# Layer one's paired blocks: one minimum from VectorE to ScalarE, weight conversion packed into five groups of eight, four subtractions to GpSimd, and 896 instead of 1,280 warming columns

## The chip, the cores and the metric

The kernel runs on one core of a Trainium2 chip, in one launch. Times are device microseconds (us) of that core, first as a median over runs without a profiler; beside them stands one execution that the hardware profiler recorded, which all rows come from. Engines are named as the profile names them: PE is TensorE's matmuls, PEld its weight loads, DVE VectorE, ACT ScalarE, POOL GpSimd, SP the queue that issues most DMAs.

## The reference

What is computed is a long convolution followed by two dense layers, each with a hidden width of 2,048:

```
X = np.fft.rfft(x, axis=1)                    # x: 2 x 3008 x 256
y = np.fft.irfft(X * F, n=3008, axis=1)       # F = filt_r + 1j * filt_i
x1 = y.reshape(6016, 256)
h = x1 @ w_in                                 # layer one, 256 -> 2048
g = np.where(h > 0, h, np.exp(np.minimum(h, 0)) - 1)
x2 = g @ w_out                                # 2048 -> 256
h2 = x2 @ w2_in                               # layer two
out = (h2 * np.clip(h2 + 3, 0, 6) / 6) @ w2_out
```

Inputs are float32, and the weights are handed over as 64-bit floats and converted on the chip.

## The kernel before, in words

**Products in three passes.** A dense product is made with operands split into a high and a low part: `mm3` (L88, L89, L90) issues three matmuls of up to 512 columns into one PSUM bank. ACT rounds the high part (L84, L559, L674), DVE subtracts it from the value for the low part (L85, L564, L679).

**Stages.** The prologue transforms the first half of the input (`s1t` L158, `tr` L171, `s2_mm` L202, `i2_mm` L222, `i1_mm` L245). Ahead of it `WARM` multiplies a tile of zeros (L1022), a list of column counts, one float32 matmul each. Then come 128 *units* (three blocks of layer one together, then five single ones), each with 12 matmuls, and last 64 *groups*. A unit's or group's extra jobs hang in slots: `at(pre, n, ...)` puts a call into slot n, a unit has one slot, a group four, and a slot's calls are issued in program order at that place. All engines run their own list in order.

**Pairs and groups.** Two blocks make a pair and share seven products instead of eight (Strassen). Layer one has two pairs, layer two six; a pair takes eight groups. Each group computes seven products (`prod`) and eight second products (`second`), 15 times three matmuls, for four hidden tiles called (0,0), (1,1), (1,0) and (0,1). Their operands are sums of input halves: `x_sums` (L548) makes four subtractions per pair, t1 to t4, and `x_high` and `x_low` (L559, L564) split them. For layer one's first pair this happens during the last single block, for the others in groups 2 to 8 of the pair before.

**The gate of layer one.** For a hidden tile h the gate is max(h, exp(min(h,0)) - 1). `add` (L634) makes h on DVE out of PSUM. For tiles in `LATE` DVE then takes min(h, 0) (L637) and `relu` issues only an exponential on ACT (L654). For others ACT takes relu(-h) (L650) and then exp of its negative (L658). `gate` (L666) joins both on DVE, `high` and `low` split the result, and `second` multiplies it.

**Conversion.** `w_chain2` is a generator that turns layer two's 64-bit weights into two float32 parts and sums of them, one piece per step: L295 to L306, L326, L373 on ACT and DVE, and L321, L330, L354, L365, L375 on POOL or DVE, as `helper` decides. `helper(1)` is POOL while the unit counter `place[0]` is from 88 to 126, DVE otherwise; the counter stops at 128 (`NU`) when groups begin. Of 101 steps, 76 are placed in units and 25 (`LEFT`) in layer one's pairs.

Of the kernel before, what the change touches and what calls it, by code (L numbers as in the profile page):

```python
# [32 lines left out]
ROUNDS = [(l, p) for l in range(2) for p in range(len(PAIRS[l]))]  # L33
# [14 lines left out]
def fft_conv_moe_moe2(ctx, tc, xp, fq, sg, cs1, cs1t, cs2, ci2, ci1, ident, w1i, w1o, w2i, w2o, out):  # L48
    nc = tc.nc
# [18 lines left out]
    def t2(shape, dt=F32):  # L68
        return p2.tile(shape, dt, tag="t2", name=name("t2"))

    def bank():
        return ps.tile([P, 512], F32, tag="ps", name=name("ps"))
# [31 lines left out]
    def got(acc, n):  # L104
        return acc[:, :n] if n == 512 else sorted_(acc[:, :n])

    def like(t, n):
        return t[:, :n] if n == 512 else halves_of(t[:, :n])
# [177 lines left out]
    def helper(layer):  # L286
        first, last = HELP[layer]
        return nc.gpsimd if first <= place[0] < last else nc.vector
# [130 lines left out]
    def w_chain2(fetch):  # L419
        bits, pending = w_words(1, 0), None  # L420
        next(bits)
        yield
        for f in range(NF + 2):
            if f < NF:
                for _ in range(2):
                    next(bits)
                    yield
                next(bits)
                if f + 1 < NF:
                    following = w_words(1, f + 1)  # L430
                    next(following)
                next(bits)
                fetch(f + 2)
                yield
                w_join(f)
                bits = following
            if 0 < f <= NF:
                w_high(f - 1)
            if pending:
                next(pending)  # L440
            yield
            if 0 < f <= NF:
                w_low(f - 1)
            if pending:
                next(pending)
                pending = None
            yield
            if f and f % 2 == 0:
                pending = w_sums(1, f // 2 - 1)
                for _ in range(2):  # L450
                    next(pending)
                    yield
# [86 lines left out]
    def x_sums(l, p, i):  # L539
        n = WIDTHS[l, p]  # L540
        if i == 0:
            xt[l, p] = [t2([P, 512]) for _ in range(4)]
        b11, b21 = (xb[l, p, 0][:, c, :n] for c in range(2))
        b12, b22 = (xb[l, p, 1][:, c, :n] for c in range(2))
        t1, t2_, t3, t4_ = (t[:, :n] for t in xt[l, p])
        out, a, b = ((t1, b12, b11), (t2_, b22, t1), (t3, b22, b12), (t4_, b21, t2_))[i]
        eng = nc.vector if (l, p) in ROUNDS[:4] else nc.gpsimd
        eng.tensor_tensor(out=out, in0=a, in1=b, op=ALU.subtract)  # L548

    def x_source(l, p, m):  # L550
# [64 lines left out]
                queue = nc.scalar if last and s else nc.sync  # L615
                queue.dma_start(out[d * P : (d + 1) * P, t0 + s : t0 + e], t[:, : e - s])

    LATE = ((0, 1), (1, 1))

    class Group:  # L620
        def __init__(self, l, p, q):
# [9 lines left out]
        def add(self, key, u, bank_):  # L631
            n = self.n
            self.h[key] = t2([P, 512])
            nc.vector.tensor_tensor(out=like(self.h[key], n), in0=got(bank_, n), in1=like(u, n), op=ALU.add)  # L634
            if not self.l and key in LATE:
                self.g[key] = t2([P, 512])
# [5 lines left out]
        def relu(self, key):  # L642
# [4 lines left out]
            if self.l:  # L647
                nc.scalar.activation(like(r, n), h, AF.Relu, bias=three)  # L648
            elif key not in LATE:
                nc.scalar.activation(like(r, n), h, AF.Relu, scale=-1.0)  # L650
# [167 lines left out]
    NU = len(units)  # L818

    NS = NU + 4 * (NF // 2) * len(ROUNDS)  # L820
    pre = [[] for _ in range(NS)]
    post = [[] for _ in range(NU + 8)]

    def at(slots, n, fn, *args):
        slots[n].append(lambda: fn(*args))
# [15 lines left out]

    WLEAD = 1

    WARM = (512, 512, 256)

# [24 lines left out]
    for n in range(NI, span):  # L872
        k = -(-n_steps * (n + 1 - NI) // (span - NI)) - done
# [8 lines left out]
    conv2 = w_chain2(fetch2)  # L882
    GROUPS = NF // 2
# [25 lines left out]
    L2 = NU + 4 * GROUPS * len(PAIRS[0])  # L909
# [5 lines left out]
    for first, last, number in ((50, 58, 10), (62, 88, 4), (88, NU - 1, 62)):  # L915
        k0 = 0
        for n in range(first, last):
            k = number * (n + 1 - first) // (last - first) - k0
# [1 line left out]
            k0 += k  # L920
        DONE += number
    LEFT = 101 - DONE
    LAST = L2 - 4
    done2 = 0
    for n in range(NU, LAST):
        k = -(-LEFT * (n + 1 - NU) // (LAST - NU)) - done2
        at(pre, n, steps, conv2, k)
        done2 += k
    for q in range(GROUPS):
        at(pre, L2 + 2 * q - 10 if q < 3 else L2 + 4 * q - 4, s_load, q)  # L930
        if q >= 3:
# [2 lines left out]
    for f in range(NF):  # L934
        at(pre, L2 + 4 * (f // 2) - (14 if f < 12 else 12 if f < 14 else 6), w_load, f)

    AHEAD = {
        0: [(x2_load, 0), (x2_load, 1)], 1: [(x_sums, 0)], 2: [(x_sums, 1), (x_part, 1)],
        3: [(x_sums, 2), (x_part, 2)], 4: [(x_sums, 3), (x_part, 5)], 5: [(x_part, 6)],
        6: [(x_part, 7), (x_part, 4)], 7: [(x_part, 3)],  # L940
    }
    LATER = [
        (2, 2, x2_load, 0), (2, 2, x2_load, 1), (3, 2, x_sums, 0), (4, 0, x_high, 1),
        (4, 1, x_low, 1), (4, 2, x_sums, 1), (5, 0, x_high, 2), (5, 1, x_low, 2),
        (5, 2, x_sums, 2), (6, 0, x_high, 6), (6, 1, x_low, 6), (6, 2, x_sums, 3),
# [64 lines left out]
    with tc.manual_schedule():  # L1010
# [9 lines left out]
        acc = bank()  # L1020
        for n in WARM:
            nc.tensor.matmul(acc[:, :n], warm[:, :P], warm[:, :n], start=True, stop=True)  # L1022
# [85 lines left out]
        n = place[0] = NU  # L1108
# [102 lines left out]
```

## Time and profile before

| what | value |
|---|---|
| median of three runs without profiler | 1055.1 us (1054.97 to 1055.27) |
| the profiled execution, its own time | 1063.18 us |
| its span, first to last instruction | 1061.4 us |
| busy in the span: PE, PEld, DVE, ACT, POOL | 99%, 87%, 83%, 75%, 19% |
| layer one's two pairs (16 groups) | from 438.2 us to 594.4 us |

The span is the time from the first to the last instruction on the engines; 1.8 us of the profiled execution's own time lie around it. Busy PE counts each matmul to its modelled end, and matmuls overlap, so 99% hides short stops; they show as the distance between the starts of two matmuls, which is 0.215 us for 512 columns where nothing stops them.

### The profile page before, as it was taken

The page shows a single profiled execution, that of the slowest core. Times are in us where ns is not written, and L with a number is a line of the kernel's source. Part 1 is how long each engine was busy: PE and PEld are TensorE (multiplying, and loading weights), DVE is VectorE, ACT ScalarE, POOL GpSimd, SP SyncE. Part 2 cuts the span into 40 slices and gives each one's busy share as a digit, 9 for nine tenths or more (in the row PEclk, how much of TensorE's full clock was granted, in tenths as well). Part 3 has the DMA queues.
Part 4 walks back from the last instruction along what each step waited for, and adds up shares of the span by engine and source line. Part 5 has one row for each costly group of instructions (what it writes and reads, how often), then busy time and mean ns, then how long its engine had stood idle before and what let it go on. Part 6 is the DMA issues. An engine that isn't in the chain of part 4 may idle for free.

```text
span 1061.4 us, 14383 instructions
## 1 busy us (share of the span) xinstructions
PE 1048.8 (99%) x5022; PEld 918.7 (87%) x5022; DVE 886.1 (83%) x1427; ACT 797.7 (75%) x1437; POOL 202.7 (19%) x218
## 2 busy tenths in 40 slices
PE   9999999999999999999999999999999999999998
PEld 7688888888889989988888888888888888888998
DVE  2899999898886799889989978888888888888776
ACT  2478888897767888877877867777777777777766
POOL 1720000444546745300021100010010010000000
PEclk9999999999999999999999999999999999999999
DMA  9785100374645454610365710100100100100100
GB/s 278 246 263 198 50 16 1 106 222 151 196 135 178 153 193 152 213 55 6 133 236 161 231 73 21 60 1 21 60 14 27 40 18 18 41 1 1 40 1 35
DMA packets 57944, 107.31 MB, mean 101 GB/s; under 512 B 5008, under 2 KB 33680, under 8 KB 57872
## 3 DMA queue, kind: packets, MB, share of 16 engines
q1 hardware_dynamic: 52144, 88.21, 25.3%
q0 software_dynamic: 4896, 17.83, 5.4%
q8 instruction: 39, 0.64, 0.3%
q10 hardware_dynamic: 832, 0.36, 0.1%
q14 instruction: 33, 0.27, 0.1%
HBM read 69.42 MB, written 36.96 MB: 100 GB/s over the span
## 4 chain that ended last, share of the span: by engine, by line
PE 82%; ACT 7%; DVE 7%; issue 2%; DMA 2%; POOL 1%; SPq 0%; DVEq 0%; ACTq 0%; POOLq 0%
PE ps L90 24%; PE ps L88 24%; PE ps L89 24%; PE ps L158 2%; PE lone L88 1%; PE lone L90 1%; PE lone L89 1%; PE ps L245 1%; DVE t L85 1%; ACT t L84 1%; DMA scr<-t 1%; POOL t L217 1%; DVE t L679 1%; PE ps L202 1%; DVE t L634 1%
## 5 line engine op out<-in xcount | busy, mean ns | idle before, releaser
L88 PE MATMUL ps<-t,w 128*128 128x512 f32 (+1 forms) x1120 | 421.2, 376 | 2.3 <-DVE t L634 1.3
L90 PE MATMUL ps<-t,w 128*128 128x512 f32 (+1 forms) x1120 | 420.2, 375 | 0.7 <-DVE t L85 0.6
L89 PE MATMUL ps<-t,w 128*128 128x512 f32 (+1 forms) x1120 | 419.6, 375 | 0.2 <-DVE w L316 0.2
L88 PEld LDWEIGHTS ps<-t,w 128*128 128x128 f32 x1120 | 211.7, 189 | 29.4 <-DVE t L498 1.9
L90 PEld LDWEIGHTS ps<-t,w 128*128 128x128 f32 x1120 | 211.6, 189 | 28.4 <-DVE t L679 2.2
L89 PEld LDWEIGHTS ps<-t,w 128*128 128x128 f32 x1120 | 211.7, 189 | 25.9 <-DVE w L316 1.6
L679 DVE TENSOR_TENSOR t<-t,t 128x512 fp32r<-128x512 f32 (+1 forms) x256 | 175.7, 701 | 24.1 <-ACT t L674 22.5
L674 ACT ACTIVATE t<-t 128x512 fp32r<-128x512 f32 (+1 forms) x256 | 154.0, 616 | 6.1 <-DVE t L664 5.7
L628 ACT ACTIVATE t<-ps 128x512 f32<-128x512 f32 (+1 forms) x176 | 103.2, 586 | 64.9 <-PE ps L90 63.3
L634 DVE TENSOR_TENSOR t<-ps,t 128x512 f32<-128x512 f32 (+1 forms) x176 | 118.1, 679 | 14.2 <-ACT t L628 13.0
L664 DVE SCALAR_TENSOR_TENSOR t<-t,t 128x512 f32<-128x512 f32 (+1 forms) x144 | 97.6, 705 | 33.3 <-ACT t L648 32.7
L648 ACT ACTIVATE t<-t,three 128x512 f32<-128x512 f32 (+1 forms) x144 | 97.2, 707 | 37.3 <-DVE t L634 36.6
L495 ACT ACTIVATE t<-ps 128x512 f32<-128x512 f32 (+1 forms) x128 | 74.1, 579 | 30.1 <-PE ps L90 28.1
L84 ACT ACTIVATE t<-t 128x512 fp32r<-128x512 f32 (+2 forms) x108 | 66.2, 618 | 22.5 <-POOL t L217 20.0
L496 ACT ACTIVATE t<-t 128x512 f32<-128x512 f32 (+1 forms) x128 | 79.3, 619 | 4.1
L85 DVE TENSOR_TENSOR t<-t,t 128x512 fp32r<-128x512 f32 (+2 forms) x96 | 73.3, 769 | 10.6 <-ACT t L84 10.4
L548 POOL TENSOR_TENSOR t<-t,t 128x512 f32<-128x512 f32 (+1 forms) x12 | 16.2, 1351 | 286.0 <-DVE t L634 257.0
L498 DVE SCALAR_TENSOR_TENSOR ps<-t,ps 128x512 f32<-128x512 f32 (+1 forms) x76 | 50.4, 663 | 23.0 <-ACT t L496 22.5
L88 PE MATMUL ps<-t,t 128*128 128x512 f32 (+1 forms) x160 | 60.2, 376 | 0.6 <-DVE t L634 0.6
L89 PE MATMUL ps<-t,t 128*128 128x512 f32 (+1 forms) x160 | 60.1, 376 | 0.0
L90 PE MATMUL ps<-t,t 128*128 128x512 f32 (+1 forms) x160 | 60.1, 376 | 0.0
L85 DVE TENSOR_TENSOR t<-ps,t 128x512 fp32r<-128x512 f32 (+1 forms) x76 | 49.9, 656 | 0.1
(115 smaller groups left out, 1520.6 us busy)
## 6 DMA issues: line engine op xcount, KB each, us to landing
t<-in_fq SPq DMA_DIRECT2D x24, 512.0 KB, 6.2
scrw<-t SPq DMA_DIRECT2D x16, 512.0 KB, 2.8
w<-scrw POOLq DMA_DIRECT2D x16, 512.0 KB, 5.0
t<-in_xp SPq DMA_DIRECT2D x16, 384.0 KB, 6.0
scr<-t SPq DMA_DIRECT2D x24, 256.0 KB, 3.0
t<-scr SPq DMA_DIRECT2D x16, 384.0 KB, 5.2
scrx<-t SPq DMA_DIRECT2D x10, 512.0 KB, 3.3
t<-scr POOLq DMA_DIRECT2D x10, 512.0 KB, 6.1
```

What stands on the lines that cost most here:

```text
L84: nc.scalar.activation(hi, src, AF.Copy)
L85: eng.tensor_tensor(out=lo, in0=src, in1=_f32(hi), op=ALU.subtract)
L88: nc.tensor.matmul(acc, wh, xh, start=start, stop=False, skip_group_check=more)
L89: nc.tensor.matmul(acc, wl, xh, start=False, stop=False, skip_group_check=more)
L90: nc.tensor.matmul(acc, wh, xl, start=False, stop=stop, skip_group_check=more)
L496: nc.scalar.activation(t[:, :n], t[:, :n], AF.Exp, scale=-1.0)
L628: nc.scalar.activation(like(t, self.n), got(bank_, self.n), AF.Copy)
L634: nc.vector.tensor_tensor(out=like(self.h[key], n), in0=got(bank_, n), in1=like(u, n), op=ALU.add)
L648: nc.scalar.activation(like(r, n), h, AF.Relu, bias=three)
L664: stt(out=r, in0=r, scalar=6.0, in1=h, op0=ALU.min, op1=ALU.mult)
L674: nc.scalar.activation(gh[:, : self.n], g[:, : self.n], AF.Copy)
L679: nc.vector.tensor_tensor(out=gl[:, :n], in0=g[:, :n], in1=_f32(gh[:, :n]), op=ALU.subtract)
```

## The change

```diff
@@ x_sums: where layer one's first-pair subtractions run
-        eng = nc.vector if (l, p) in ROUNDS[:4] else nc.gpsimd
+        eng = helper(1) if (l, p) in ROUNDS[:4] else nc.gpsimd
@@ tiles whose minimum VectorE takes
-    LATE = ((0, 1), (1, 1))
+    LATE = ((0, 1),)
@@
-    WARM = (512, 512, 256)
+    WARM = (512, 384)
@@ the 25 conversion steps of layer one's pairs
-    LAST = L2 - 4
-    done2 = 0
-    for n in range(NU, LAST):
-        k = -(-LEFT * (n + 1 - NU) // (LAST - NU)) - done2
-        at(pre, n, steps, conv2, k)
-        done2 += k
+    calm = [NU + 4 * GROUPS * r + k for r in range(2) for k in range(20)]
+    for i in range(LEFT):
+        at(pre, calm[i * len(calm) // LEFT], steps, conv2, 1)
```

`helper(1)` is POOL only for the first pair's four subtractions, which are issued in units 102, 106, 110 and 114; for the other pairs of `ROUNDS[:4]` the counter stands at 128 and DVE keeps them. Tile (1,1) leaves `LATE` in layer one's two pairs, 16 groups: DVE issues 16 minima (L637) less, and ACT issues a relu (L650) and an exponential (L658) where it issued one exponential (L654). The 25 conversion steps were spread over 60 of the 64 slots; now 13 stand in the first 20 slots (five groups) of the first pair and 12 in those of the second.

On VectorE, in the sixth group of the first pair, from the gate of tile (0,0) to the add of tile (0,1), before:

```order
L666 SCALAR_TENSOR_TENSOR t_1259_5255<-t_1259_5255,lone_5221 128x512
L679 TENSOR_TENSOR t_1262_5263<-t_1249_5218,t_1261_5260 128x512
L304 TENSOR_SCALAR t_1193_4976<-t_1192_4975 128x512
L306 SCALAR_TENSOR_TENSOR t_1194_4977<-raw_4667,t_1193_4976 128x512
L564 TENSOR_TENSOR t_1256_5246<-t_845_3392,t_1256_5246 128x512
L634 TENSOR_TENSOR t_1268_5288<-ps_5222,t_1263_5277 128x512
L637 TENSOR_SCALAR t_1269_5290<-t_1268_5288 128x512
L679 TENSOR_TENSOR t_1270_5292<-t_1259_5255,t_1267_5286 128x512
L548 TENSOR_TENSOR t_1224_5094<-t_851_3422 128x512
L666 SCALAR_TENSOR_TENSOR t_1269_5290<-t_1269_5290,t_1268_5288 128x512
L634 TENSOR_TENSOR t_1272_5317<-ps_5222,t_1257_5251 128x512
```

The same stretch in the changed kernel:

```order
L666 SCALAR_TENSOR_TENSOR t_1264_5268<-t_1264_5268,lone_5234 128x512
L679 TENSOR_TENSOR t_1267_5276<-t_1254_5231,t_1266_5273 128x512
L564 TENSOR_TENSOR t_1261_5259<-t_845_3391,t_1261_5259 128x512
L634 TENSOR_TENSOR t_1270_5295<-ps_5235,t_1268_5290 128x512
L679 TENSOR_TENSOR t_1271_5297<-t_1264_5268,t_1269_5293 128x512
L548 TENSOR_TENSOR t_1227_5102<-t_851_3421 128x512
L666 SCALAR_TENSOR_TENSOR t_1272_5299<-t_1272_5299,t_1270_5295 128x512
L634 TENSOR_TENSOR t_1274_5324<-ps_5235,t_1262_5264 128x512
```

Two conversion instructions (L304, L306) and the minimum (L637) are gone; a third conversion instruction, L321, is gone further down in the same group.

On ScalarE, in the same group, from the copy of the sixth product's bank to the relu of tile (1,0), before:

```order
L628 ACTIVATE t_1263_5277<-ps_5220 128x512
L295 ACTIVATE t_1264_5280<-raw_4980 128x512
L674 ACTIVATE t_1267_5286<-t_1259_5255 128x512
L654 ACTIVATE t_1269_5290<-t_1269_5290 128x512
L650 ACTIVATE t_1271_5309<-ps_5220 128x512
```

and in the changed kernel:

```order
L628 ACTIVATE t_1268_5290<-ps_5233 128x512
L674 ACTIVATE t_1269_5293<-t_1264_5268 128x512
L650 ACTIVATE t_1272_5299<-t_1270_5295 128x512
L658 ACTIVATE t_1272_5299<-t_1272_5299 128x512
L650 ACTIVATE t_1273_5316<-ps_5233 128x512
```

The exponential L654 that waited for DVE's minimum became the pair L650 and L658, which read the add's result; the conversion's L295 moved to an earlier group.

On POOL, in units 104 to 110, before:

```order
L330 TENSOR_TENSOR t_1019_4182<-t_957_3922,t_1019_4182 128x512
L375 TENSOR_TENSOR t_1020_4184<-t_995_4072,t_1020_4184 128x512
L321 TENSOR_TENSOR t_1008_4145<-t_1008_4145,t_1010_4147 128x512
L330 TENSOR_TENSOR t_1037_4269<-t_986_4038,t_1037_4269 128x512
L365 TENSOR_TENSOR t_1043_4297<-t_986_4038 128x128
```

and in the changed kernel:

```order
L330 TENSOR_TENSOR t_1019_4181<-t_957_3921,t_1019_4181 128x512
L375 TENSOR_TENSOR t_1020_4183<-t_995_4071,t_1020_4183 128x512
L548 TENSOR_TENSOR t_980_4012<-t_833_3348 128x512
L321 TENSOR_TENSOR t_1008_4144<-t_1008_4144,t_1010_4146 128x512
L330 TENSOR_TENSOR t_1037_4268<-t_986_4037,t_1037_4268 128x512
L365 TENSOR_TENSOR t_1043_4296<-t_986_4037 128x128
```

The third subtraction stands right behind L375; the other three are put in the same way, each ahead of an L321.

## Rows read from the trace of the kernel before

**Rows 1.** Busy time by stretch: first five and last three groups of each pair.

```profile
438.20:485.20 47.00, 47.00 (x220) 41.08 (x219) 41.05 (x75) 35.83 (x67) 2.90 (x6) 1.00 0.33 111
485.20:516.70 31.50, 30.75 (x140) 25.63 (x139) 28.90 (x53) 25.31 (x48) 1.58 (x3) 1.00 0.19 59
516.70:565.20 48.50, 48.46 (x223) 41.51 (x222) 44.65 (x79) 37.95 (x72) 7.04 (x13) 1.00 0.61 210
565.20:594.40 29.20, 29.13 (x135) 25.15 (x134) 26.34 (x47) 24.20 (x46) 4.76 (x10) 1.00 0.53 163
```

**Rows 2.** Waits of the weight loads, 484 to 519 us: total, times, longest.

```profile
PEld ps L90 <- DVE t L679: 1.1, 3, 0.5
PEld ps L88 <- DVE t L634: 1.0, 1, 1.0
PEld lone L88 <- ACT lone L750: 0.4, 1, 0.4
```

**Rows 3.** Timeline of PE, 493 to 495 us: start, length, instruction.

```profile
493.42 0.38 PE L90 MATMUL ps<-t,w 128*128 128x512 f32 x1
494.44 0.48 PE L88 MATMUL ps<-t,t 128*128 128x512 f32 x1 [0.65 <-DVE t L634]
```

**Rows 4.** Waits of the weight loads, 438 to 484 us.

```profile
PEld ps L90 <- DVE t L679: 0.5, 2, 0.3
```

**Rows 5.** Timeline of all engines, 590 to 597 us, the last group's end.

```profile
592.15 0.43 DVE L637 TENSOR_SCALAR t<-t 128x512 f32<-128x512 f32 x1
...
592.61 0.63 ACT L654 ACTIVATE t<-t 128x512 f32<-128x512 f32 x1 [0.98 <-DVE t L637]
...
593.70 0.69 DVE L666 SCALAR_TENSOR_TENSOR t<-t,t 128x512 f32<-128x512 f32 x1
...
593.95 0.38 PE L90 MATMUL ps<-t,w 128*128 128x512 f32 x1
...
594.30 0.69 DVE L564 TENSOR_TENSOR t<-t,t 128x512 fp32r<-128x512 f32 x1
...
594.90 0.69 DVE L634 TENSOR_TENSOR t<-ps,t 128x512 f32<-128x512 f32 x1
...
595.64 0.48 PE L88 MATMUL ps<-t,w 128*128 128x512 f32 x1 [1.31 <-DVE t L634]
```

**Rows 6.** Groups of instructions, 438.2 to 594.4 us: busy, mean ns, idle before.

```profile
L654 ACT ACTIVATE t<-t 128x512 f32<-128x512 f32 x31 | 19.5, 629 | 22.1 <-DVE t L637 21.8
L658 ACT ACTIVATE t<-t 128x512 f32<-128x512 f32 x31 | 19.4, 627 | 0.5
...
L637 DVE TENSOR_SCALAR t<-t 128x512 f32<-128x512 f32 x31 | 13.2, 427 | 1.3
...
L650 ACT ACTIVATE t<-lone 128x512 f32<-128x512 f32 x16 | 9.4, 588 | 0.0
```

**Rows 7.** Timeline of DVE, 393 to 441 us.

```profile
395.05 0.41 DVE L297 TENSOR_SCALAR t<-t 128x512 f32<-128x512 f32 x1
...
399.26 0.67 DVE L548 TENSOR_TENSOR t<-t 128x512 f32<-128x512 f32 x1
...
412.26 1.25 DVE L297 TENSOR_SCALAR t<-t 128x512 f32<-128x512 f32 x1
413.55 1.39 DVE L298 TENSOR_SCALAR t<-t 128x512 uint32<-128x512 uint32 x1
```

**Rows 8.** Timeline of POOL, 380 to 440 us.

```profile
393.37 1.28 POOL L375 TENSOR_TENSOR t<-t,t 128x512 fp32r<-128x512 f32 x1
399.41 1.65 POOL L321 TENSOR_TENSOR t<-t,t 128x512 f32<-128x512 f32 x1 [4.76 <-DVE t L306]
...
411.95 1.28 POOL L330 TENSOR_TENSOR t<-t,t 128x512 fp32r<-128x512 f32 x1
413.18 1.46 POOL L375 TENSOR_TENSOR t<-t,t 128x512 fp32r<-128x512 f32 x1
```

**Rows 9.** Timeline of PE, 415 to 416.5 us.

```profile
415.14 0.35 PE L89 MATMUL ps<-t,w 128*128 128x448 f32 x1
416.05 0.46 PE L90 MATMUL ps<-t,w 128*128 128x448 f32 x1 [0.56 <-DVE t L85]
```

**Rows 10.** Timeline of all engines, 0 to 22 us.

```profile
1.32 4.63 PE L1022 MATMUL ps<-warm 128*128 128x512 f32 x6 [1.32 <-POOL warm L1019]
...
6.49 13.94 PE L158 MATMUL ps<-s1t,t 96*128 96x96 f32 x64 [0.53 <-DMA t<-in_xp]
```

**Rows 11.** The chain that ended last, 6 to 43 us: start, length, what.

```profile
1.19 5.17 DMA t<-in_xp
...
35.66 3.32 PE ps L158 x30
```

## The prediction

> **What bounds the kernel now.** I read the page first, then the busy times by stretch, then the waits of the weight loads and the timelines at the places they point to. PE bounds the kernel: it is hardly ever idle, so a change on DVE or ACT can only give back the short stops in which a matmul waits for them, or add new ones. The stretch that the change touches is layer one's two pairs. There the four rows by stretch [rows 1] say how near DVE is to being a second bound: in the first five groups of the first pair it is busy for 41.05 of 47.00 us (87%), in the last three for 28.90 of 31.50 (92%), then 44.65 of 48.50 (92%) and 26.34 of 29.20 (90%). ACT runs at 76%, 80%, 78% and 83% there. PE's own stops stand where DVE is fullest: from 484 to 519 us weight loads wait for DVE four times, 1.1 + 1.0 = 2.1 us, and once 0.4 us for ACT [rows 2], but only 0.5 us in all before that [rows 4]. A weight load runs ahead of its matmul, so not all of that is lost. The longest, 1.0 us, shows what is: the matmul starts come 494.44 - 493.42 = 1.02 us apart where 0.215 is the undisturbed distance, so 0.81 us are lost [rows 3]. At the same 0.8 the 2.1 us are 1.7 us of lost PE time. A second stop stands at the passage to layer two: starts at 593.95 and 595.64, 1.69 - 0.215 = 1.48 us lost to an add on DVE [rows 5].
>
> **The change part by part.**
>
> *Conversion out of groups 6 to 8.* In the sixth group of the first pair DVE issues 13 instructions instead of 17, in the seventh 13 for 17 and in the eighth 17 for 18. Where DVE is full, instructions follow each other every 0.60 us (593.70, 594.30, 594.90 [rows 5]), so four less, one of them a minimum of 0.43 us [rows 6], free 3 x 0.60 + 0.43 = 2.2 us in a group of 9.7. None of the stops here was longer than 1.0 us [rows 2]. I take 1.5 of the 1.7 us as given back: **-1.5 us** (bounds 0 and -1.7).
>
> *The passage to layer two.* The eighth group of the second pair loses its minimum (592.15, 0.43 us) and the groups before it some conversions. The chain that ends in the stop is gate 593.70, subtraction 594.30, add 594.90, matmul 595.64 [rows 5], all on DVE and shifted forward together by what is gone. The gate itself must wait for its exponential, which before ended at 592.61 + 0.63 = 593.24; now a relu of 0.59 us [rows 6] starts where the minimum did, 592.15, and the exponential of 0.63 follows, so it ends at about 593.37. The gate can thus come 0.33 us earlier and no more. The conversions that are gone may bring the add before it forward too; I take **-0.6 us** (bounds -0.3 and -1.48).
>
> *The minimum itself.* Over the 16 groups DVE loses 16 x 0.427 = 6.8 us and ACT gains 16 x 0.588 = 9.4 us of relu; the exponential stays, as L658 instead of L654 [rows 6]. ACT goes from 123.3 us in 156.2, summed over the four stretches [rows 1], to 132.7, 85%: still under PE. What the path sees is the chain from add to gate: before 0.43 + 0.63, now 0.59 + 0.63, 0.16 us longer. It hides where DVE has another instruction between, as it does in the group whose rows stand above (L679 and L548), and shows where it has none.
>
> *Conversion into groups 1 to 5.* 25 steps now fall into 40 slots; before, evenly spread over 60, those 40 held 16 to 17. DVE gets up to two instructions more in a group there (13 to 14, 15 to 16, 14 to 16 in those that gain), less one minimum each. The first pair's five groups can take it: 41.05 of 47.00 us were busy. The second pair's are at 92%. I add **+0.4 us** for new short stops: ten groups with 0.04 each as the middle between none and the whole 0.16 of the longer chain (bounds 0 and +1.6).
>
> *Four subtractions to POOL.* They leave DVE (0.67 us each, with 0.60 to the next [rows 7]) where it runs without a pause. POOL takes 1.28 us for such an instruction [rows 8], and was idle from 394.65 to 399.41, so it has room; the operands are needed nine or more units later, so nobody waits for them. But POOL and DVE disturb each other: L297 takes 0.41 us alone (395.05) and 1.25 at 412.26, L298 1.39 at 413.55 [rows 7], while POOL runs L330 and L375 [rows 8], and a matmul then starts 0.91 us after the one before instead of 0.19, 0.72 us lost [rows 9]. In the new order the third subtraction stands behind L375 and will run at 394.65 to 395.93, on top of the L297 of 395.05: about 0.84 us lost on DVE against 0.60 won. The fourth, and the earlier conversion chain behind it, shorten the collision at 412 us, since POOL's L321 waits for a DVE instruction that comes 0.6 us earlier. Together I take **-0.3 us** (bounds: -0.72, and +1.0 for four collisions of 0.84 less four times 0.60).
>
> The Trainium skill (SBUF — State Buffer, section Who interferes with whom) speaks against this part: it says that VectorE in its two-port modes and GpSimd share a port pair that is held for a whole instruction, so that the later one fully blocks. The slow L297 and L298 agree with it, and by the rule taken strictly all four subtractions that meet such an instruction cost their whole 1.28 us, which would make the sum 0.3 to 3 us worse than mine.
>
> *Warming columns.* The six records of the warming block take 4.63 us from 1.32 on, and the first real matmul starts at 6.49, behind a wait for its input [rows 10], which lands at 1.19 + 5.17 = 6.36 [rows 11]. 384 columns of 1,280 are 30%, 1.3 us. The block ends earlier and PE waits longer for the same landing: **0 us** in this profile, hidden by the DMA. If the input landed at once, up to 0.5 us could be won.
>
> **The sum.** -1.5 - 0.6 + 0.4 - 0.3 = -2.0 us: the profiled execution, 1063.18 us with a span of 1061.4, would become 1061.2 with a span of 1059.4. The median without profiler is 8.1 us lower, and I carry the difference over: **1053.1 us**. About 0.2% (2.1 us) is what a measurement of this kernel can tell from no change, so the forecast lies at that border.
>
> **Where the 8.1 us may come from**, since a rival hangs on it. The first 64 L158 matmuls take 13.94 us, 218 ns each [rows 10]; 30 of the same at 35.66 take 3.32 us, 111 ns each [rows 11]. So the first ran at the lower of the clock's two levels (1.2 GHz) and the later at the upper (2.4 GHz), though the clock column reads 1.00 throughout; the 4.63 us of warming did not raise it in this execution. At the later distance the 64 would take 7.1 us, 6.9 less. Runs without profiler may well have had the clock up by then.
>
> **The rivals.**
>
> *The clock rises too late (slower).* If the 1055.1 us contain an early rise that the long warming block brought, a block of 3.3 us with a gap of 1.8 us behind it may not bring it. Then the 64 matmuls cost 6.9 us more, and the time is 1055.1 - 2.0 + 6.9 = 1060.0. It decides as soon as over 4.1 us of the 6.9 are lost. For it: the 8.1 us. Against it: the one execution shown did not profit from even the long block. Chance 0.12. The Trainium skill (TensorE: Matmul & The Clock Gate, section Part 1: The HAM clock gate) states that the engine starts throttled, that sustained activity releases it and that the moment varies from run to run, which fits this rival; no row before shows an early rise.
>
> *ScalarE's longer chain is felt everywhere.* If in all 16 groups the gate comes 0.16 us later and PE waits for it, 2.6 us eat the gain: 1055.7. For it: DVE waits for exponentials at its gates already, and ACT is at 83% in the last groups. Against: PE hardly stopped in groups 1 to 5. Chance 0.16, with tails on the slower side.
>
> *The subtractions collide.* With +1.0 instead of -0.3 the time is 1054.4. Chance 0.10.
>
> *All stops go.* 1.7 + 1.48 + 0.72 and the 0.5 of warming are 4.4 us: 1050.7. Chance 0.08.
>
> **How the numbers follow.** My forecast, 1053.1 with a range of its own from 1051.4 to 1054.7, has 0.54. Its larger half-width is the passage (0.9) and the five groups (1.2). Faster by over 0.2% is a little over half of it and nearly all of the last rival, with the collision case giving some: 0.44. Slower by over 0.2%: the clock and a tail of ScalarE's chain: 0.16. Within 0.2%: 0.40. The range is 1050.4 to 1056.4; it takes in all cases but the clock's and tails.
>
> **What would show it.** Right: from 484 to 519 us the waits for L679 and L634 fall from 2.1 to under 0.5; the last L637 before the passage is gone and the matmul that followed L634 comes less than 0.9 us late; L658 counts 16 more and L650 too; no wait of PE for DVE longer than 0.3 us in the first five groups of a pair; the first L158 still starts when its input lands. Wrong: waits for L666 or L658 between 440 and 485 or 517 and 565; L297 at over 1 us beside an L548 on POOL; 64 L158 matmuls at another distance than 218 ns, or a time near 1060.

## The result and the profile after

The changed kernel takes 1061.67 us (median of 20 runs, 1054.28 to 1062.89), the kernel before 1054.96 (20 runs, 1054.30 to 1058.09). The ratio is 1.0051, 95% interval 1.0037 to 1.0064: slower by half a per cent, and by 6.7 us between the medians. The runs of the changed kernel fall into groups, and the number can't be understood without them: 3 of 20 lie at 1054.3 to 1054.5, 4 at 1059.6 to 1059.9 and 13 at 1061.2 to 1062.9. Of the kernel before, 19 of 20 lie at 1054.3 to 1055.6.

The profiled execution after is one of the long ones (1062.89 us, span 1061.1). So was that of before: with 1063.18 us it lies 8 us above nearly all of its kernel's runs. Busy time by engine, from the page:

```profile
PE 1048.7 (99%) x5020; PEld 918.6 (87%) x5020; DVE 878.9 (83%) x1407; ACT 807.6 (76%) x1453; POOL 208.0 (20%) x222
```

Busy time in layer one's pairs after, in the same four stretches as [rows 1] (columns: stretch, its length, then busy time of PE, PEld, DVE, ACT and POOL):

```profile
438.80:486.70 47.90, 47.85 (x221) 40.70 (x220) 41.98 (x75) 40.11 (x75) 2.90 (x6) 1.00 0.35 120
486.70:516.30 29.60, 29.60 (x139) 25.75 (x138) 25.42 (x44) 25.82 (x50) 1.69 (x3) 1.00 0.12 36
516.30:565.30 49.00, 48.60 (x225) 41.89 (x224) 43.39 (x77) 41.75 (x79) 6.87 (x13) 1.00 0.63 215
565.30:594.40 29.10, 29.05 (x135) 25.11 (x133) 24.58 (x41) 25.28 (x48) 4.84 (x10) 1.00 0.56 163
```

The last three groups of the first pair got 1.9 us shorter (31.50 to 29.60), the first five 0.9 longer (47.00 to 47.90), and the second pair's first five 0.5 longer; the four together went from 156.2 to 155.6. The groups of instructions after, in the pairs, beside [rows 6]:

```profile
L658 ACT ACTIVATE t<-t 128x512 f32<-128x512 f32 x47 | 29.5, 628 | 1.0
...
L650 ACT ACTIVATE t<-t 128x512 f32<-128x512 f32 x16 | 10.1, 630 | 14.5 <-DVE t L634 14.5
...
L637 DVE TENSOR_SCALAR t<-t 128x512 f32<-128x512 f32 x15 | 6.4, 428 | 0.5
```

16 minima less and 16 relus more, at 0.63 us each where 0.59 was taken. Nothing here is 6.7 us. The passage to layer two, timeline after, beside [rows 5]:

```profile
593.42 0.69 DVE L666 SCALAR_TENSOR_TENSOR t<-t,t 128x512 f32<-128x512 f32 x1 [0.16 <-ACT t L658]
...
593.97 0.38 PE L90 MATMUL ps<-t,w 128*128 128x512 f32 x1
...
595.37 0.48 PE L88 MATMUL ps<-t,w 128*128 128x512 f32 x1 [1.02 <-DVE t L634]
```

The gate now waits 0.16 us for its exponential, and the matmul comes 1.40 us after the one before instead of 1.69. The start of the kernel, timeline of PE after, beside [rows 10]:

```profile
1.32 3.35 PE L1019 MATMUL ps<-warm 128*128 128x512 f32 x4 [1.32 <-POOL warm L1016]
5.97 13.94 PE L158 MATMUL ps<-s1t,t 96*128 96x96 f32 x64 [1.30 <-DMA t<-in_xp]
```

The 64 first matmuls take 13.94 us, as in the profiled execution of before; PE's pause ahead of them has grown from 0.53 to 1.30 us. These two profiles alone show hardly any difference, because both caught the late case.

Below, *stops* means PE time lost in a stretch: for each two successive matmuls the distance of their starts less 0.216 us (512 columns) or 0.192 (448), summed where it is over 0.02.

### The profile page after: what moved, and what is told of

Same layout as the page of the kernel before. It is cut to its first block, busy times and chain, and to the rows that moved or that the text cites. A ratio compares the mean times of both kernels' runs of the same rounds, so it can differ in the third digit from the quotient of the medians.

```text
span 1061.1 us, 14393 instructions
## 1 busy us (share of the span) xinstructions
PE 1048.7 (99%) x5020; PEld 918.6 (87%) x5020; DVE 878.9 (83%) x1407; ACT 807.6 (76%) x1453; POOL 208.0 (20%) x222
## 4 chain that ended last, share of the span: by engine, by line
PE 88%; ACT 5%; DVE 3%; DMA 2%; issue 1%; POOL 0%; SPq 0%; DVEq 0%; ACTq 0%
PE ps L90 26%; PE ps L88 26%; PE ps L89 26%; PE ps L158 2%; PE lone L88 2%; PE lone L90 2%; PE lone L89 2%; PE ps L245 1%; ACT t L84 1%; DMA scr<-t 1%; PE ps L202 1%; PE ps L222 1%; ACT t L495 1%; PE ps L171 1%; DVE t L85 1%
## 5 line engine op out<-in xcount | busy, mean ns | idle before, releaser
L88 PE MATMUL ps<-t,w 128*128 128x512 f32 (+1 forms) x1120 | 421.2, 376 | 2.0 <-DVE t L634 1.0
L88 PEld LDWEIGHTS ps<-t,w 128*128 128x128 f32 x1120 | 211.7, 189 | 28.8 <-DVE t L498 2.1
L85 DVE TENSOR_TENSOR t<-t,t 128x512 fp32r<-128x512 f32 (+2 forms) x96 | 72.5, 759 | 10.7 <-ACT t L84 10.4
L548 POOL TENSOR_TENSOR t<-t,t 128x512 f32<-128x512 f32 (+1 forms) x15 | 20.1, 1342 | 286.2 <-DVE t L634 257.0
L88 PE MATMUL ps<-t,t 128*128 128x512 f32 (+1 forms) x160 | 60.2, 376 | 0.0
L85 DVE TENSOR_TENSOR t<-ps,t 128x512 fp32r<-128x512 f32 (+1 forms) x76 | 49.7, 654 | 0.1
```

What stands on the lines that cost most here:

```text
L85: eng.tensor_tensor(out=lo, in0=src, in1=_f32(hi), op=ALU.subtract)
L88: nc.tensor.matmul(acc, wh, xh, start=start, stop=False, skip_group_check=more)
```

## The experiments

Two theories stood against each other at first. *Clock*: the short warming block leaves the first 64 matmuls at the lower of TensorE's two clock levels in most executions. *Pairs*: ScalarE's longer chain and new stops in the groups cost the time.

**The changed kernel with the old block.**

```diff
-    WARM = (512, 384)
+    WARM = (512, 512, 256)
```

> The changed kernel with the old warming block of 1,280 columns. Theory clock (the short block leaves the first 64 matmuls of the transform at the lower clock level in most executions): 1054.2 us, 0.8 under the kernel before, since the stops of PE in the two profiles differ by 27.7 - 26.8 = 0.9 us; the 64 matmuls about 111 ns apart in undisturbed executions. Theory pairs (the longer chain on ScalarE and the new stops in the paired groups cost the 6.7 us): about 1061.7 us, as the changed kernel.

Measured: 1054.15 us (12 runs; 11 at 1053.7 to 1054.8, one at 1062.28), ratio 0.9995 (0.9977 to 1.0014). The three other edits are worth 0.8 us by the medians (1054.94 for the kernel before beside it), as the clock theory had it; the interval does not tell that from no change. Theory pairs falls. This profile caught an early rise. Timeline of PE, the start:

```profile
1.32 4.63 PE L1019 MATMUL ps<-warm 128*128 128x512 f32 x6 [1.32 <-POOL warm L1016]
5.75 7.50 PE L158 MATMUL ps<-s1t,t 96*128 96x96 f32 x64
13.97 1.50 PE L171 MATMUL ps<-id,zt 128*128 128x128 f32 x12 [0.73 <-DVE zt L81]
```

The 64 matmuls take 7.50 us instead of 13.94: 0.11 us apart from the fourth on, instead of 0.21, the upper of the levels 1.2 and 2.4 GHz. The 12 transposes after them take 1.50 instead of 2.82. PE starts its real work without a pause behind the block, as the input lands before the block ends. Dense matmuls begin 8.7 us earlier (first L88 at 56.65 for 65.37 in the profile of the changed kernel) and the span is 1052.3 for 1061.1: all of it comes through to the end.

**The kernel before with the short block.**

```diff
-    WARM = (512, 512, 256)
+    WARM = (512, 384)
```

> The kernel before with nothing changed but the warming block, 896 columns for 1,280. Theory clock: about 1062.4 us in most runs (1061.7 + 0.7), with a few near 1055. Theory pairs: 1055.0 us, no change.

Measured: 1062.46 us (8 runs, 1060.16 to 1063.85, none early; three of them, at 1060.2 to 1061.2, with a mean granted clock of 0.994), against 1054.94, ratio 1.0062 (1.0042 to 1.0081). This line alone costs 7.5 us by the medians. Its profile, timeline of PE:

```profile
1.32 3.35 PE L1022 MATMUL ps<-warm 128*128 128x512 f32 x4 [1.32 <-POOL warm L1019]
5.80 13.94 PE L158 MATMUL ps<-s1t,t 96*128 96x96 f32 x64 [1.13 <-DMA t<-in_xp]
```

**No block.**

```diff
-    WARM = (512, 512, 256)
+    WARM = ()
```

> The kernel before without any warming matmul. Theory clock: every execution late, 1062 to 1064 us, and no run near 1055; the 64 matmuls 213 ns apart in the profile. Theory pairs: 1055 us.

Measured: 1062.81 us (6 runs, 1062.49 to 1063.03), ratio 1.0067 (1.0044 to 1.0089). No run is early. The short block is thus hardly better than none, and the 64 matmuls do not raise the clock by themselves: 13.94 us here too.

**A longer block, and one between.**

```diff
-    WARM = (512, 512, 256)
+    WARM = (512, 512, 512, 256)   # warm_1792
+    WARM = (512, 512)             # warm_1024
```

> The kernel before with a longer block, 1,792 columns, which at the distances of the profile ends 1.3 us after the first input has landed. Theory clock: every execution early, the median 1055.0 plus 0 to 1.3 us for the later start, no run above 1057. Theory pairs: the same median, as nothing in the pairs differs; it is the spread of the runs that is of interest.

> The kernel before with a block of 1,024 columns, between the two. Both theories expect a mixture: some runs near 1055 and some from 1059 to 1063, more early ones than with 896 columns (3 of 20 in the changed kernel) and fewer than with 1,280 (44 of 45 so far are under 1059).

Measured: with 1,792 columns 1055.55 us (12 runs, 1054.17 to 1056.28, all early), ratio 1.0000 (0.9987 to 1.0013); with 1,024 columns 1055.12 (12 runs: eight at 1054.0 to 1055.2, four at 1062.4 to 1063.4), ratio 1.0020 (0.9995 to 1.0044). So it is a matter of chance from run to run, and the length moves the chance: none of 6 with no block, 3 of 20 and 0 of 8 with 896 columns, 8 of 12 with 1,024, all but 4 of 122 with 1,280 (the kernel before in all its sets), 12 of 12 with 1,792. The longest holds up the first matmul to 7.09 us and its median is 0.6 us higher.

**The short block, later.** Is it too short, or is the pause behind it the trouble?

```diff
-    WARM = (512, 512, 256)
+    WARM = (512, 384)
...
-            nc.tensor.matmul(acc[:, :n], warm[:, :P], warm[:, :n], start=True, stop=True)
+            nc.tensor.matmul(acc[:KP, :n], mats["s1t"], warm[:, :n], start=True, stop=True)
```

> The kernel before with the short block of 896 columns, whose weights are the transform's 128x96 matrix instead of zeros, so that it starts when that matrix lands (3.08 us in the profile of before) instead of at 1.32, and ends near the landing of the first input. It computes nothing that is used, as before. Theory gap (the pause of 1.1 to 1.3 us behind the short block is what loses the early rise): most runs near 1055, plus up to 0.6 for a later first matmul. Theory length (896 columns are too few wherever they stand): most runs near 1062.

Measured: 1055.72 us (12 runs: seven at 1054.6 to 1055.8, five at 1063.2 to 1063.4), ratio 1.0028 (1.0004 to 1.0053). Its profile, timeline of PE:

```profile
2.89 3.20 PE L1022 MATMUL ps<-warm,s1t 128*96 128x512 f32 x4 [2.89 <-DMA s1t<-in_cs1t]
5.92 2.26 PE L158 MATMUL ps<-s1t,t 96*128 96x96 f32 x19
```

The same 896 columns, from 2.89 instead of 1.32 us and with no pause behind them: 7 of 12 early instead of 3 of 28. So the place of the block counts as well as its length, as 5 of 12 were late and few are with 1,280 columns. That it is the pause is likely but not shown: the edit also starts the block later and gives it another weight matrix, and no run takes these apart. A pause does not by itself exclude an early rise. The profiled execution with 1,024 columns is early, with 0.90 us of pause:

```profile
6.00 7.60 PE L158 MATMUL ps<-s1t,t 96*128 96x96 f32 x64 [0.90 <-DMA t<-in_xp]
```

That of before, late, has 1,280 columns and only 0.53 us of pause [rows 10].

**One part at a time: the subtractions.**

```diff
-        eng = nc.vector if (l, p) in ROUNDS[:4] else nc.gpsimd
+        eng = helper(1) if (l, p) in ROUNDS[:4] else nc.gpsimd
```

> The kernel before with only the first pair's four subtractions on POOL. The prediction's term: -0.3 us, 1054.6. Rival (the subtractions collide with VectorE's conversion instructions, as the profile of the changed kernel suggests: the stops of PE between 375 and 420 us sum to 1.45 us there and to 1.35 before): +0.1 us or more, 1055.0 to 1055.9, with L297 or L298 at over 1 us beside an L548 on POOL.

Measured: 1055.21 us (11 runs) against 1055.08 (33 runs, of which one took 1063.32 and one 2841.4), ratio 1.0000 (0.9991 to 1.0009). No gain. The timelines of POOL and DVE of this run show why (all its times lie about 8 us under those of [rows 7]):

```profile
385.39 1.29 POOL L375 TENSOR_TENSOR t<-t,t 128x512 fp32r<-128x512 f32 x1
386.63 1.68 POOL L548 TENSOR_TENSOR t<-t 128x512 f32<-128x512 f32 x1
```

```profile
387.09 1.50 DVE L297 TENSOR_SCALAR t<-t 128x512 f32<-128x512 f32 x1
...
392.76 0.68 DVE L85 TENSOR_TENSOR t<-ps,t 128x512 fp32r<-128x512 f32 x1
```

and the same L85 in the kernel before:

```profile
400.45 0.68 DVE L85 TENSOR_TENSOR t<-ps,t 128x512 fp32r<-128x512 f32 x1
```

The third subtraction runs behind L375, as foreseen, and the L297 beside it takes 1.50 us instead of 0.41. From the start of this L297 to the start of that L85, DVE takes 5.67 us instead of 5.40 (from 395.05 to 400.45 in the kernel before), though the subtraction of 399.26 between them is gone. The matmul that waits for this L85 is thus held up more, not less (0.59 us lost against 0.43), the one of [rows 9] less (0.45 against 0.72).

**One part at a time: the minimum.**

```diff
-    LATE = ((0, 1), (1, 1))
+    LATE = ((0, 1),)
```

> The kernel before with only the minimum of tile (1,1) taken from VectorE (relu and exponential on ScalarE). The prediction's terms: -0.3 to -0.6 us at the passage to layer two and a part of the 1.5 us in groups 6 to 8 of the first pair, together about -1.0, 1053.9. Rival (ScalarE's chain, 0.16 us longer in each group, comes through to PE): 0 to +2.6 us, 1055 to 1057.5, with more waits of PE for L679 in all groups.

Measured: 1053.14 us (11 runs, 1052.88 to 1054.37) against 1055.08, ratio 0.9977 (0.9962 to 0.9992). This edit alone gains 1.9 us by the medians, nearly what all four were forecast to bring. Together with the conversion and the subtractions it brought 0.8 (1054.15 against 1054.94). Stretches of its profile:

```profile
429.50:476.50 47.00, 47.00 (x220) 41.05 (x219) 39.73 (x71) 38.70 (x72) 2.91 (x6) 1.00 0.33 111
476.50:506.80 30.30, 30.03 (x138) 25.74 (x138) 27.57 (x49) 26.92 (x50) 1.59 (x3) 1.00 0.18 60
506.80:555.30 48.50, 48.50 (x224) 41.90 (x224) 42.96 (x74) 41.10 (x77) 7.02 (x13) 1.00 0.62 212
555.30:584.50 29.20, 29.13 (x135) 25.16 (x134) 25.23 (x44) 25.79 (x49) 4.77 (x10) 1.00 0.51 163
```

Against [rows 1] the last three groups of the first pair are 1.2 us shorter, and no stretch is longer. Its stops from the first group to the passage sum to 2.6 us, those of before to 4.1: 1.4 of the 1.9 us are found there.

**One part at a time: the conversion.**

```diff
-    LAST = L2 - 4
-    ...
+    calm = [NU + 4 * GROUPS * r + k for r in range(2) for k in range(20)]
+    for i in range(LEFT):
+        at(pre, calm[i * len(calm) // LEFT], steps, conv2, 1)
```

> The kernel before with only the conversion steps packed into five groups of each pair. The prediction's terms: -1.2 in groups 6 to 8, +0.6 in groups 1 to 5 without the freed minimum: -0.6 us, 1054.3. Rival (the new stops in groups 3 to 5 and in the second pair, 0.4 + 0.7 us in the profile of the changed kernel, are its own and grow without the freed minimum): 0 to +1.5, 1055 to 1056.5.

Measured: 1055.50 us (11 runs, one of them late at 1063.36) against 1055.08, ratio 1.0010 (0.9995 to 1.0024): no gain. In its profile the stops of the last three groups of the first pair fall from 1.66 us to 0.31, and those of the first five rise from 0.19 to 1.41. It moves the stops.

**Both edits of the pairs.**

```diff
-    LATE = ((0, 1), (1, 1))
+    LATE = ((0, 1),)
...
+    calm = [NU + 4 * GROUPS * r + k for r in range(2) for k in range(20)]
...
```

> Both edits of the pairs, the old warming block, subtractions on VectorE. If the subtractions on POOL gave nothing or cost a little: at or up to 0.5 us under the kernel with all three edits and the old block, 1053.7 to 1054.2. If they gave the predicted 0.3: 1054.5.

Measured: 1054.34 us (11 runs) against 1055.08, ratio 0.9992 (0.9983 to 1.0001); stops 0.98 us in the first five groups, 0.10 in the last three, 0.83 in the second pair's first five and 1.28 at the passage, 3.2 in all. By the medians it lies 1.2 us above the minimum alone, and its stops are 0.6 us more. The intervals of the two ratios overlap, so the size is not settled, but nothing speaks for a gain from packing the conversion. Whether the subtractions add anything (1054.15 with them) these medians can't tell.

**Both minima to ScalarE.**

```diff
-    LATE = ((0, 1), (1, 1))
+    LATE = ()
```

> The kernel before with both of layer one's minima taken from VectorE: tile (0,1) too gets relu and exponential on ScalarE. If VectorE's load alone makes the stops: another part of the 2.6 us of stops left with one minimum gone, 1052 to 1052.8. If ScalarE's longer chain then comes through (it goes to about 91% busy in the last groups): 1053.1 to 1055.

Measured: 1059.97 us (12 runs, 1059.44 to 1060.69), ratio 1.0042 (1.0030 to 1.0055), 5.0 us slower, far over what was expected. What DVE waited for in the pairs, in this run and then in the run with one minimum moved (total, times, longest):

```profile
DVE t L666 <- ACT t L658: 21.8, 49, 1.9
```

```profile
DVE t L666 <- ACT t L658: 12.6, 29, 1.9
```

and PE, again in this run and then in the other:

```profile
PEld ps L90 <- DVE t L679: 6.7, 19, 0.5
```

```profile
PEld ps L90 <- DVE t L679: 0.9, 3, 0.3
```

The gate waits for the exponential 9 us more, and PE in turn for the split that follows the gate, 19 times in 16 groups instead of 3. PE's stops from the first group to the passage sum to 9.0 us where before has 4.1, so they account for the 5.0. ScalarE is busy for 140.2 of 160.8 us in the pairs, 87%: not full, but its chain is on the path. Whether that comes from the second minimum as such or from the place of tile (0,1) in the group, no run separates: (0,1) was not moved alone.

**The best version with a block of 1,536 columns.**

```diff
-    WARM = (512, 512, 256)
+    WARM = (512, 512, 512)
```

> The best version so far (only the minimum of tile (1,1) moved) with a block of 1,536 columns. If a longer block makes the early rise surer at no cost: 1053.1 us and no run above 1056. If it costs by holding up the first matmul, as 1,792 columns did (+0.6): up to 1053.7.

Measured: 1053.48 us (11 runs: ten at 1052.9 to 1054.0, one at 1205.11 with a mean granted clock of 0.851, which the ratio leaves out) against 1054.95, ratio 0.9986 (0.9976 to 0.9995). Better than both kernels, 0.3 us above the same with 1,280 columns; that the longer block makes the early rise surer can't be told from so few runs of each, none of which was at 1062.

## Why the prediction was wrong, step by step

*Warming columns: the step that failed.* "The block ends earlier and PE waits longer for the same landing: 0 us in this profile, hidden by the DMA." That holds for an execution in which the clock rises late anyway, and the profiled one was such. The other executions were the median's: there the long block raises the clock ahead of the 64 matmuls, the short one mostly does not, and the cost is 7.5 us. The rival with this mechanism was worked out (1060.0 us: 6.9 us for the 64 matmuls, less the forecast gain of 2.0, of which 0.8 came) and got a chance of 0.12. The evidence for it was in the table: 8.1 us between the profiled execution and the median, of which the 64 matmuls at the upper level explain 6.9 and nothing else was found to explain any. It should have been the likeliest case for what the median contains. The size was also short: 12 transposes (1.3 us) and the first transforms behind them run at the lower level too.

*ScalarE's chain.* It does not bind with one minimum moved: in the changed kernel DVE's waits for L658 grow from 8.0 to 13.2 us, which the prediction had named as a sign of being wrong, but PE's waits for DVE in the pairs fall from 4.8 to 3.6. With both minima moved it binds.

*The minimum: mis-attributed.* Outside the passage the prediction gave it no gain of its own and booked the relief in groups 6 to 8 to the conversion steps that leave them. Alone it gains 1.9 us, and takes stops out of three of the four places where they stood (1.66 to 0.72, 0.65 to 0.37, passage 1.58 to 1.28).

*Conversion out of groups 6 to 8* was right in place and size: -1.5 us forecast, and stops that fell from 1.66 to 0.10 us in the changed kernel. *Into groups 1 to 5* was mis-sized: +0.4 us forecast, +0.8 in the first pair and +0.2 in the second measured, inside the stated bounds (up to 1.6). With the passage and the subtractions, below, that is why the sum without the clock is -0.8 and not -2.0.

*The passage*: -0.6 us forecast, -0.3 measured, the bound that the sum itself had worked out from the exponential; the 0.3 more that were taken on top had no row. The matmul behind the add still came 1.18 us late, where under 0.9 was named as a sign of being right.

*The subtractions*: -0.3 us forecast, +0.1 measured by the medians, which is no difference. The third does what the text said (L297 at 1.50 us), and the 1.09 us of DVE time that it loses there are more than the 0.60 that the one instruction saves. The Trainium skill (SBUF — State Buffer, section Who interferes with whom) had warned of it: VectorE in its two-port modes and GpSimd exclude each other for a whole instruction. The trace agrees with 1.50 us for an instruction of 0.41 that met one of 1.68.

What stays open: why four executions of the changed kernel lie at 1059.6 to 1059.9 us. Their mean granted clock is 0.994, as in three of the kernel before with the short block (1060.2 to 1061.2 us) and nearly so in a fifth of the changed kernel (0.992, 1061.19 us); all other runs whose clock is on record have 0.999 to 1.0, but for the one at 1205.11 us. All eight have the 896 columns that start at 1.32 us. By estimate 0.994 of a 1,058 us span is some 13 us at half the clock, which would fit a clock that rose early and fell again, but none of the eight was traced.

## What to carry to other kernels

Compare the profiled execution's own time with the median before reading anything from it: a gap of several us says that the profile caught another case, and any edit near the place that can explain the gap must be costed for the case that the median holds. A warming block is worth what follows it at the upper clock level, here 7.5 us. Don't trim it on the evidence of one profile: here fewer columns gave fewer early runs, and so did the same columns further ahead of the first real matmul. Judge it by how many runs come out early. When two edits relieve the same stretch, neither can be given the relief by argument; run each alone, since here one brought 1.9 us and the other, by the medians, took 1.2 of it back (a size that the intervals leave open).

## What the runs showed of the hardware that had not been expected

The clock's rise is a matter of chance per execution, and the warming block shifts the chance: with 896 columns 3 of 28 runs were early, with 1,024 columns 8 of 12, with 1,792 12 of 12, and with 896 columns placed 1.57 us later, up against the first matmuls, 7 of 12. The Trainium skill (TensorE: Matmul & The Clock Gate, section Part 1: The HAM clock gate) says that sustained activity releases the throttle and that the moment varies between runs; the second agrees with these counts. The first does not account for the late executions: there the 64 transform matmuls ran 213 ns apart and without a gap for 13.9 us, and the clock did not rise. It rose while PE was at the transposes and transforms behind them (213 ns per transpose at 20.5 us and 109 ns at 27 us in the profile of the changed kernel). And the clock column of the profile reads 1.00 in both cases, so the level has to be read from the distance between matmuls. The reason is that the trace's clock record begins only at the rise. In the ten early profiles it begins between 4.6 and 7.5 us, in the four late ones between 23.0 and 26.3, and in none between.
